# Rounding float64 weights with one VectorE shift and three ScalarE operations, and a subtraction of one moved from VectorE to ScalarE

## The chip, the cores and the metric

The kernel runs on one core of a Trainium2 chip. The metric is the device time of one execution in microseconds (us); three executions of the kernel before were timed, and a fourth was recorded by the hardware profiler. The engines are named as the profile names them: PE is TensorE (PEld its weight loads), DVE is VectorE, ACT is ScalarE, POOL is GpSimd, SP is SyncE, which here only issues DMAs. Each engine takes its instructions in the order in which the program wrote them.

## The reference

Three layers follow one another on 8 sequences of 3072 tokens with 256 channels: a filter in the frequency domain, a soft mixture of experts, and a gated feed-forward layer. Cut to what matters:

```python
X = np.fft.rfft(x, axis=1)
y = np.fft.irfft(X * (filt_r + 1j * filt_i)[None], n=seq, axis=1)      # layer 1
logits = y @ phi                                                       # layer 2
d = softmax(logits over tokens); slot_input = d.T @ y                  # 32 slots, 8 experts
slot_out[e] = relu(slot_input[e] @ w1[e]) @ w2[e]
z = softmax(logits over slots) @ slot_out
g = z @ w_gate                                                         # layer 3
out = (g * sigmoid(g) * (z @ w_val)) @ w_out
```

The three weights of layer 3 (`w_gate`, `w_val`: 256 x 1536; `w_out`: 1536 x 256) are given as float64, everything else as float32. The kernel computes in float32, so these weights are rounded to float32 on the chip.

## The kernel before, in words

**Stage 1** (`phase1`, to about 412 us of the profiled execution) does the transforms. The work is a list of 96 units: 16 steps (a step is one half of the channels of one of the 8 sequences) of 6 units each. For each unit `s2_unit` does 16 matmuls into a PSUM tile `X`, two DVE products `P` and `Q` read from it, and POOL combines them to `y`; two units later `tr_unit` transposes `y` on PE into `T`, ACT copies it to `yt`, and `phi_pair` multiplies with `phi` into `L`. In four of six units `s1_chunk` does a chunk of the next step's first transform: PE writes the PSUM tile `s` (L217), DVE transposes it to `sg` (L225), and `spread` copies that on ACT to `b` (L234), which the next step's `X` matmuls read. The tile `s` has one buffer, so the next chunk's matmuls wait until DVE has read the one before.

Beside the units run two generators, each advanced by one `yield` at a time. `pump` advances `chain(b, last)` by one step a unit: it turns the logits of sequence `b` into slot inputs. Its steps, in order, are `lh` and `us` (evacuations on ACT), `t4` (two transposes on DVE), `lg` (two ACT copies, L396) with `cm` (two DVE reductions L397 and a maximum L398), a PE transpose of `cm` (L407), `mg`, `mb`, `dg` (small DVE operations), `dd` (two DVE subtractions L420 and two ACT exponentials L426), the subtraction of one from `dd` (L430, two on DVE), PE matmuls over `dd` (L438), two DVE transposes to `bd` (L347), PE matmuls over `bd` (L450), and so on. `aside` advances `conv`, two steps a unit, which rounds the weights; when that is used up it advances `first_weights`.

`conv` works on 36 chunks of 128 x 256 weights, four steps a chunk. SP loads a chunk as pairs of 32-bit words into `raw` (two buffers; the load for chunk n+2 is issued behind the store of chunk n). Step 1: DVE takes the exponent `ex` and the mantissa's high part `mn` from the high words (L584, L585). Step 2: ACT scales the exponent, the low words and the mantissa (L587 to L589). Step 3: DVE joins sign and exponent (L591). Step 4: POOL adds and multiplies (L593, L594), and SP stores the result in DRAM and issues the next load.

**Transition and stage 2.** Then the experts run on 32 slots (`transition`, to about 454 us), behind loads of their weights that begin when stage 1 has freed its memory, and stage 2 (`phase2`) does the gated layer to the end.

Of the kernel before, what the change touches and what calls it, by code (L numbers as in the profile page):

```python
# [7 lines left out]
F32 = mybir.dt.float32  # L8
F32R = mybir.dt.float32r
I32 = mybir.dt.int32  # L10
U32 = mybir.dt.uint32
AF = mybir.ActivationFunctionType
ALU = mybir.AluOpType
# [66 lines left out]
def spectral_softmoe_glu_kernel(  # L80
# [18 lines left out]
    pe, dve, act, pool = nc.tensor, nc.vector, nc.scalar, nc.gpsimd  # L99
# [13 lines left out]
    expo = const.tile([128, 1], F32, name="expo")  # L113
# [17 lines left out]
    def phase1():  # L131
        with ExitStack() as c1:
# [5 lines left out]
            cvp = c1.enter_context(tc.tile_pool(name="cvp", bufs=1))  # L138
# [168 lines left out]
            def chain(b, last):  # L307
# [33 lines left out]
                def col(t, k, n=128):  # L341

                    w = 512 // n
                    return t[k // w][:, k % w * n:(k % w + 1) * n]
# [6 lines left out]
                for k in range(6):  # L351
                    pe.transpose(
                        out=col(ps, k),
# [6 lines left out]
                for jj in range(NJ):  # L360
                    g, k = jj % 4, jj // 4
                    pe.matmul(
                        out=col(ps, k)[32 * g:32 * g + 32],
# [23 lines left out]
                for h in range(2):  # L387
                    for g in range(2):
                        pe.matmul(
                            out=pl[h][64 * g:64 * g + 64].rearrange("p (e n) -> p e n", n=16),  # L390
# [9 lines left out]
                for h in range(2):  # L400
                    for g in range(2):
                        nc.sync.dma_start(
                            out=lgd[b].rearrange("(n h) g e k -> h g n e k", h=2)[h, g],
# [6 lines left out]
                    out=mg, in_=ps[0:32, 0:128].rearrange("p (g n) -> p g n", g=2)[:, :, 0:48], axis=AX.X, op=ALU.max  # L410
# [7 lines left out]
                dd = chp.tile([128, 2, E, 16], F32, tag="t4", name="dd")  # L418
                for h in range(2):
                    dve.tensor_tensor(  # L420
                        out=dd[:, h],
                        in0=lg[h],
                        in1=pm[:, :, None].to_broadcast([128, E, 16]),
                        op=ALU.subtract,
# [2 lines left out]
                if not last:  # L427
                    yield
                for h in range(2):
                    dve.tensor_scalar_add(dd[:, h], dd[:, h], -1.0)  # L430
                yield
                bd = chp.tile([128, E, 32], F32, tag="lg", name="bd")
                pl = (ps_s1.tile([128, 1024], F32, tag="s1", name="cl") if last else small()).rearrange(
# [2 lines left out]
                for g in range(2):  # L436
                    for h in range(2):
                        pe.matmul(  # L438
                            out=pl[64 * h:64 * h + 64, g],
# [8 lines left out]
                for jj in range(NJ):  # L448
                    g, k = jj % 4, jj // 4
                    pe.matmul(  # L450
                        out=col(ps, k)[32 * g:32 * g + 32],
# [26 lines left out]
                for q in range(3):  # L478
                    for ri in range(2):
                        for g in range(4):  # L480
                            pe.matmul(  # L481
                                out=ps[32 * g:32 * g + 32, 0:D],
# [17 lines left out]
                if last:  # L500
                    pe.matmul(
                        out=pss[96:128, :], lhsT=rb[:, b, :], rhs=sl, start=False, stop=True, tile_position=(0, 96)
# [52 lines left out]
            def flat(a):  # L555
                return a.rearrange("(p a) f -> p (a f)", p=128)

            def conv():


                cw = 256
                chunks = [(i, c) for i in range(3) for c in range(FF * D // 128 // cw)]
                raws = {}

                def load(n):
                    if n >= len(chunks):
                        return
                    i, c = chunks[n]
                    raws[n] = cvp.tile([128, cw, 2], I32, tag="raw", name="raw", bufs=2)
                    nc.sync.dma_start(  # L570
                        out=raws[n].rearrange("p n k -> p (n k)"),
                        in_=flat((w_gate, w_val, w_out)[i])[:, c * cw:(c + 1) * cw].bitcast(I32),
                    )

                load(0)
                load(1)
                yield
                for n, (i, c) in enumerate(chunks):
                    raw = raws.pop(n)
                    hw, lw, lf = raw[:, :, 1], raw[:, :, 0].bitcast(U32), raw[:, :, 0].bitcast(F32)  # L580
                    ex = cvp.tile([128, cw], I32, tag="ex", name="ex", bufs=2)
                    mn = cvp.tile([128, cw], I32, tag="mn", name="mn", bufs=2)
                    mf = mn.bitcast(F32)
                    dve.tensor_scalar(ex, hw, 20, 0x7FF, ALU.logical_shift_right, ALU.bitwise_and)  # L584
                    dve.tensor_scalar(mn, hw, 0xFFFFF, 0x100000, ALU.bitwise_and, ALU.bitwise_or)  # L585
                    yield
                    act.activation(ex, ex, AF.Relu, bias=expo, scale=float(1 << 23))  # L587
                    act.activation(lf, lw, AF.Copy, scale=2.0 ** -32)
                    act.activation(mf, mn, AF.Copy)  # L589
                    yield  # L590
                    dve.scalar_tensor_tensor(ex, hw, -(1 << 31), ex, ALU.bitwise_and, ALU.bitwise_or)  # L591
                    yield
                    pool.tensor_tensor(out=mf, in0=mf, in1=lf, op=ALU.add)  # L593
                    pool.tensor_tensor(out=mf, in0=mf, in1=ex.bitcast(F32), op=ALU.mult)  # L594
                    nc.sync.dma_start(out=flat(wd[i])[:, c * cw:(c + 1) * cw], in_=mf)
                    load(n + 2)
                    yield
# [54 lines left out]
                        spread()  # L652
            xp += [cr.enter_context(tc.tile_pool(name=f"xp{k}", bufs=1, side="right")) for k in (1, 0)][::-1]
            dve.memset(ones, 1.0)
            dve.memset(expo, -916.0 * (1 << 23))
            side = [conv(), first_weights()]
            todo = []
            gens, ready = [], []
# [18 lines left out]
            def tail_ops(i):  # L677
                if 0 <= i - 2 < len(units):
                    tr_unit(*units[i - 2])
                if i - 4 >= 0 and i % 2 == 0 and i - 3 < len(units):  # L680
                    s, u = units[i - 4]
                    phi_pair(s, u // 2)
                    if s % 2 == 1 and u == 4:
                        ready.append((s // 2, chain(s // 2, s // 2 == NB - 1)))
# [352 lines left out]
    with tc.manual_schedule():  # L1037
        phase1()
        phase2(transition())
        p2.close()  # L1040
# [32 lines left out]
```

## Time and profile before

| | us |
|---|---|
| three timed executions | 1542.36, 1543.30, 1543.52 (median 1543.3) |
| span of the profiled execution | 1537.9 |
| what the median has beyond that span | 5.4 |
| busy in the profiled execution: PE, DVE, ACT, POOL | 1449.9, 1204.9, 955.1, 241.3 |
| end of stage 1, end of the transition | about 412, about 454 |

The profile gives the profiled execution's time as its span alone; the 5.4 us between this and the median of the timed runs lies outside the span. Busy times are averages over stages with different limits, so a change in stage 1 has to be read in stage 1.

### The profile page before, as it was taken

The page shows a single profiled execution, that of the slowest core. Times are in us where ns is not written, and L with a number is a line of the kernel's source. Part 1 is how long each engine was busy: PE and PEld are TensorE (multiplying, and loading weights), DVE is VectorE, ACT ScalarE, POOL GpSimd, SP SyncE. Part 2 cuts the span into 40 slices and gives each one's busy share as a digit, 9 for nine tenths or more (in the row PEclk, how much of TensorE's full clock was granted, in tenths as well). Part 3 has the DMA queues.
Part 4 walks back from the last instruction along what each step waited for, and adds up shares of the span by engine and source line. Part 5 has one row for each costly group of instructions (what it writes and reads, how often), then busy time and mean ns, then how long its engine had stood idle before and what let it go on. Part 6 is the DMA issues. An engine that isn't in the chain of part 4 may idle for free.

```text
span 1537.9 us, 26707 instructions
## 1 busy us (share of the span) xinstructions
PE 1449.9 (94%) x10282; PEld 1133.8 (74%) x10282; DVE 1204.9 (78%) x1976; ACT 955.1 (62%) x1808; POOL 241.3 (16%) x297
## 2 busy tenths in 40 slices
PE   3789998898869999999999999999999999999998
PEld 1455555555438888888888888888888888888887
DVE  3698899898328878887887788788778878877775
ACT  2365565564227666766766677677667667666665
POOL 1566555654010000000000000000000000000000
PEclk9999999999989999999999999999999999999999
DMA  9978678761990120121112013101301310120111
GB/s 193 189 132 147 115 132 142 124 117 56 366 279 25 35 68 19 29 69 27 27 35 71 16 28 69 30 23 35 72 15 29 69 35 18 35 62 14 28 29 28
DMA packets 90482, 116.53 MB, mean 76 GB/s; under 512 B 8657, under 2 KB 69970, under 8 KB 90034
## 3 DMA queue, kind: packets, MB, share of 16 engines
q1 hardware_dynamic: 88882, 111.15, 33.2%
q10 hardware_dynamic: 1216, 3.15, 1.1%
q8 instruction: 81, 1.33, 0.4%
q0 software_dynamic: 256, 0.52, 0.2%
q14 instruction: 47, 0.39, 0.1%
HBM read 68.13 MB, written 34.60 MB: 67 GB/s over the span
## 4 chain that ended last, share of the span: by engine, by line
PE 80%; DVE 11%; DMA 5%; issue 2%; ACT 1%; SPq 1%; POOL 0%; DVEq 0%; ACTq 0%; POOLq 0%
PE o L987 35%; PE o L991 18%; PE V L960 9%; PE G L959 9%; PE X L248 2%; DVE sg L225 2%; DVE P L256 2%; PE s L217 2%; DVE Q L257 2%; DMA fwd<-in_const_fwd_dram 2%; DMA raw<-in_moe_w_gate_dram 1%; PE T L279 1%; PE c L481 1%; DMA w<-in_moe_w_dram 1%; PE L L288 1%
## 5 line engine op out<-in xcount | busy, mean ns | idle before, releaser
L987 PE MATMUL o<-wo,hi 128*128 128x512 f32 x2304 | 831.1, 395 | 0.0
L991 PE MATMUL o<-wo,lo 128*128 128x256 f32 x2304 | 644.6, 280 | 0.2 <-DVE lo L976 0.2
L962 ACT ACTIVATE s<-G 128x512 f32<-128x512 f32 x576 | 344.7, 598 | 317.4 <-PE G L959 314.5
L968 DVE TENSOR_TENSOR h<-V,s 128x512 f32<-128x512 f32 x576 | 395.2, 686 | 168.9 <-ACT s L962 168.1
L987 PEld LDWEIGHTS o<-wo,hi 128*128 128x128 f32 x2304 | 432.0, 187 | 103.4
L991 PEld LDWEIGHTS o<-wo,lo 128*128 128x128 f32 x2304 | 433.6, 188 | 25.9 <-DVE lo L976 0.6
L976 DVE TENSOR_TENSOR lo<-h,hi 128x512 fp32r<-128x512 f32 x576 | 417.1, 724 | 0.1
L975 ACT CAST hi<-h 128x512 fp32r<-128x512 f32 x576 | 354.7, 616 | 12.5 <-DVE h L968 9.2
L960 PE MATMUL V<-c,v 128*128 128x512 f32 x576 | 227.4, 395 | 2.1 <-DVE h L968 1.8
L959 PE MATMUL G<-c,g 128*128 128x512 f32 x576 | 227.9, 396 | 0.0
L248 PEld LDWEIGHTS X<-b,fwd 128*64 128x64 f32 x1536 | 83.2, 138 | 67.9 <-issue 50.2
L959 PEld LDWEIGHTS G<-c,g 128*128 128x128 f32 x576 | 108.1, 188 | 25.6 <-issue 0.8
L234 ACT COPY b<-sg 128x768 f32<-128x768 f32 x64 | 58.7, 918 | 102.6 <-DVE sg L225 102.3
L225 DVE STREAM_TRANSPOSE sg<-s 128x1024 f32<-128x1024 f32 x64 | 78.9, 1236 | 47.9 <-PE s L217 47.9
L248 PE MATMUL X<-b,fwd 128*64 128x128 f32 x1536 | 106.3, 281 | 10.5 <-ACT b L234 5.0
L960 PEld LDWEIGHTS V<-c,v 128*128 128x128 f32 x576 | 108.6, 189 | 4.2 <-DVE h L968 2.9
L906 POOL TENSOR_TENSOR lg<-lg,mx 96x1024 f32<-96x1024 f32 x7 | 16.9, 2418 | 581.1 <-DVE mx L904 581.1
L217 PE MATMUL s<-x,csm 48*64 48x512 f32 x512 | 73.3, 628 | 34.2 <-DMA x<-in_x_dram 21.1
L1001 DVE TENSOR_TENSOR ot<-o,tmp 128x256 f32<-128x256 f32 x192 | 70.0, 423 | 39.5 <-ACT tmp L1000 39.5
L269 POOL TENSOR_TENSOR y<-P 128x256 f32<-128x256 f32 x96 | 70.2, 731 | 144.5 <-DVE P L256 144.5
L271 POOL TENSOR_TENSOR y<-Q 128x256 f32<-128x256 f32 x95 | 77.4, 815 | 0.9 <-DVE Q L259 0.8
L281 ACT COPY yt<-T 128x512 f32<-128x512 f32 x96 | 55.9, 582 | 30.4 <-PE T L279 29.9
(195 smaller groups left out, 1017.6 us busy)
## 6 DMA issues: line engine op xcount, KB each, us to landing
out_dram<-ot SPq DMA_DIRECT2D x192, 128.0 KB, 2.2
x<-in_x_dram SPq DMA_DIRECT2D x56, 384.0 KB, 8.2
w<-in_moe_w_dram SPq DMA_DIRECT2D x16, 1024.0 KB, 12.4
c<-ch SPq DMA_DIRECT2D x42, 128.0 KB, 2.4
c<-cl SPq DMA_DIRECT2D x42, 128.0 KB, 2.4
raw<-in_moe_w_gate_dram SPq DMA_DIRECT2D x12, 256.0 KB, 4.5
lgd<-lg SPq DMA_DIRECT2D x32, 96.0 KB, 6.9
raw<-in_moe_w_val_dram SPq DMA_DIRECT2D x12, 256.0 KB, 3.7
```

The lines of the kernel that those rows point to most:

```text
L217: pe.matmul(out=ps[64 * k:64 * k + 64, 16 * r:16 * r + 16, :], lhsT=s1t_sb[64 * r:64 * r + 48, :], rhs=xt[step][64 * r:64 * r + 48, k, :, ...
L225: dve.transpose(out=sg.rearrange("p j d k -> p d j k"), in_=ps.rearrange("p n d -> p d n"))
L248: pe.matmul(out=ps[par * 64:(par + 1) * 64, i, ri, :], lhsT=fwd[:, j, ri * 64:(ri + 1) * 64], rhs=bb[:, j, :],)
L271: eng.tensor_tensor(out=y[:, :, 1, :], in0=Q[:, :, 0, :], in1=Q[:, :, 1, :], op=ALU.add)
L959: pe.matmul(out=pg, lhsT=g4[c][:, fs], rhs=c4[b][:, q, G, :])
L960: pe.matmul(out=pv, lhsT=v4[c][:, fs], rhs=c4[b][:, q, G, :])
L962: act.activation(s, pg, AF.Silu)
L968: dve.tensor_tensor(out=h, in0=pv, in1=s, op=ALU.mult)
L975: act.copy(hi, h)
L976: dve.tensor_tensor(out=lo, in0=h, in1=hi, op=ALU.subtract)
L987: pe.matmul(out=a, lhsT=hi[:, ts], rhs=wo[f].rearrange("p k d -> p (k d)"), start=(f == 0), stop=(f == NF - 1), skip_group_check=True,)
L991: pe.matmul(out=a[:, D:2 * D], lhsT=lo[:, ts], rhs=wo[f][:, 0, :], start=False, stop=(f == NF - 1), skip_group_check=True,)
```

## The change

The rounding of a chunk is done in another way, still in four steps. Step 1: ACT reads the high words as float32 and scales them, which moves the exponent, into `mag`. Step 2: ACT scales the low words into an integer `low` of 0 to 8, and writes the sign of the high words over them. Step 3: DVE shifts `mag` left by three bits, which drops the old sign. Step 4: POOL adds `low` to `mag` as integers, and multiplies with the sign. So DVE has one operation a chunk and not three, ACT three as before, POOL two as before with an integer add. The subtraction of one in `chain` goes to ACT for the seven sequences that are not the last.

```diff
                 for h in range(2):
-                    dve.tensor_scalar_add(dd[:, h], dd[:, h], -1.0)
+                    if last:
+                        dve.tensor_scalar_add(dd[:, h], dd[:, h], -1.0)
+                    else:
+                        act.activation(dd[:, h], dd[:, h], AF.Copy, bias=-1.0)
                 yield
...
                     raw = raws.pop(n)
-                    hw, lw, lf = raw[:, :, 1], raw[:, :, 0].bitcast(U32), raw[:, :, 0].bitcast(F32)
-                    ex = cvp.tile([128, cw], I32, tag="ex", name="ex", bufs=2)
-                    mn = cvp.tile([128, cw], I32, tag="mn", name="mn", bufs=2)
-                    mf = mn.bitcast(F32)
-                    dve.tensor_scalar(ex, hw, 20, 0x7FF, ALU.logical_shift_right, ALU.bitwise_and)
-                    dve.tensor_scalar(mn, hw, 0xFFFFF, 0x100000, ALU.bitwise_and, ALU.bitwise_or)
-                    yield
-                    act.activation(ex, ex, AF.Relu, bias=expo, scale=float(1 << 23))
-                    act.activation(lf, lw, AF.Copy, scale=2.0 ** -32)
-                    act.activation(mf, mn, AF.Copy)
-                    yield
-                    dve.scalar_tensor_tensor(ex, hw, -(1 << 31), ex, ALU.bitwise_and, ALU.bitwise_or)
-                    yield
-                    pool.tensor_tensor(out=mf, in0=mf, in1=lf, op=ALU.add)
-                    pool.tensor_tensor(out=mf, in0=mf, in1=ex.bitcast(F32), op=ALU.mult)
+                    hf, lw = raw[:, :, 1].bitcast(F32), raw[:, :, 0].bitcast(U32)
+                    mag = cvp.tile([128, cw], I32, tag="mag", name="mag", bufs=2)
+                    low = cvp.tile([128, cw], I32, tag="low", name="low", bufs=2)
+                    act.activation(mag.bitcast(F32), hf, AF.Copy, scale=2.0 ** -112)
+                    yield
+                    act.activation(low, lw, AF.Copy, scale=2.0 ** -29)
+                    act.activation(hf, hf, AF.Sign)
+                    yield
+                    dve.tensor_scalar(mag, mag, 3, None, ALU.logical_shift_left)
+                    yield
+                    pool.tensor_tensor(out=low, in0=mag, in1=low, op=ALU.add)
+                    mf = low.bitcast(F32)
+                    pool.tensor_tensor(out=mf, in0=mf, in1=hf, op=ALU.mult)
                     nc.sync.dma_start(out=flat(wd[i])[:, c * cw:(c + 1) * cw], in_=mf)
```

On DVE, this is the stretch of one sequence's chain from `cm` to the transpose behind `dd`, before and then after; the numbers on `s` tell one tile from the next.

```order
L584 TENSOR_SCALAR ex<-raw 128x256
L585 TENSOR_SCALAR mn<-raw 128x256
L397 TENSOR_REDUCE cm<-lg 128x32 x2
L398 TENSOR_TENSOR cm<-cm 128x32
L256 TENSOR_TENSOR P<-X,ft 128x512
L257 TENSOR_TENSOR Q<-X,ft 128x512
L591 SCALAR_TENSOR_TENSOR ex<-raw,ex 128x256
```

```order
L397 TENSOR_REDUCE cm<-lg 128x32 x2
L398 TENSOR_TENSOR cm<-cm 128x32
L256 TENSOR_TENSOR P<-X,ft 128x512
L257 TENSOR_TENSOR Q<-X,ft 128x512
L591 TENSOR_SCALAR mag<-mag 128x256
L409 TENSOR_REDUCE mg<-c 32x2
```

The pair `ex`, `mn` ahead of `cm` is gone, and the shift stands where the join of sign and exponent stood, directly behind `Q`.

Further on in the same chain, on DVE, from `dg` to the transposes `bd`, before and then after:

```order
L414 TENSOR_SCALAR dg<-csm,mb 32x32
L225 STREAM_TRANSPOSE sg<-s_2226 128x32x16x2
L256 TENSOR_TENSOR P<-X,ft 128x512
L257 TENSOR_TENSOR Q<-X,ft 128x512
L584 TENSOR_SCALAR ex<-raw 128x256
L585 TENSOR_SCALAR mn<-raw 128x256
L420 TENSOR_TENSOR dd<-lg,c 128x512 x2
L225 STREAM_TRANSPOSE sg<-s_2279 128x32x16x2
L256 TENSOR_TENSOR P<-X,ft 128x512
L257 TENSOR_TENSOR Q<-X,ft 128x512
L591 SCALAR_TENSOR_TENSOR ex<-raw,ex 128x256
L430 TENSOR_SCALAR dd<-dd 128x512 x2
```

```order
L414 TENSOR_SCALAR dg<-csm,mb 32x32
L225 STREAM_TRANSPOSE sg<-s_2190 128x32x16x2
L256 TENSOR_TENSOR P<-X,ft 128x512
L257 TENSOR_TENSOR Q<-X,ft 128x512
L420 TENSOR_TENSOR dd<-lg,c 128x512 x2
L225 STREAM_TRANSPOSE sg<-s_2242 128x32x16x2
L256 TENSOR_TENSOR P<-X,ft 128x512
L257 TENSOR_TENSOR Q<-X,ft 128x512
L591 TENSOR_SCALAR mag<-mag 128x256
L225 STREAM_TRANSPOSE sg<-s_2277 128x32x16x2
```

One `ex`, `mn` pair ahead of `dd` and both subtractions ahead of the next `sg` are gone.

On ACT at the same place, before and then after:

```order
L426 ACTIVATE dd<-dd 128x512 x2
L587 ACTIVATE ex<-ex,expo 128x256
L588 ACTIVATE raw<-raw 128x256
L589 ACTIVATE mn<-mn 128x256
L234 COPY b<-sg 128x24x32
L281 COPY yt<-T 128x512
L234 COPY b<-sg 128x24x32
```

```order
L586 ACTIVATE mag<-raw 128x256
L426 ACTIVATE dd<-dd 128x512 x2
L588 ACTIVATE low<-raw 128x256
L589 ACTIVATE raw<-raw 128x256
L234 COPY b<-sg 128x24x32
L281 COPY yt<-T 128x512
L433 ACTIVATE dd<-dd 128x512 x2
L234 COPY b<-sg 128x24x32
```

The scaling into `mag`, the first reader of the loaded `raw`, now stands on ACT ahead of the exponentials, and the two subtractions stand between `yt` and the next `b`. Nothing else changes its place on PE, POOL or SP.

## Rows read from the trace of the kernel before

**Rows 1.** The page, its first line.

```profile
span 1537.9 us, 26707 instructions
```

**Rows 2.** Windows: length, busy us (instructions) by engine, clock, DMA; one repeat, five summed.

```profile
177.99:224.03 46.04, 41.74 (x541) 24.94 (x537) 42.11 (x71) 26.69 (x58) 27.01 (x37) 1.00 0.81 135
...
sum 230.21, PE 208.72 PEld 124.76 DVE 210.89 ACT 133.89 POOL 135.45; mean PE 41.74 PEld 24.95 DVE 42.18 ACT 26.78 POOL 27.09
```

**Rows 3.** PE's waits in four repeats, 131.93 to 316.10 us.

```profile
PE s L217 <- DVE sg L225: 6.3, 4, 1.6
PE c L450 <- DVE bd L347: 4.2, 4, 1.0
PE c L407 <- DVE cm L398: 4.0, 4, 1.0
PE X L248 <- ACT b L234: 1.9, 4, 0.5
```

**Rows 4.** PE in order of time, one repeat: start, us, what, idle before.

```profile
188.61 0.27 PE L407 MATMUL c<-csm,cm 128*32 128x128 f32 x1 [1.01 <-DVE cm L398]
...
196.61 1.09 PE L217 MATMUL s<-x,csm 48*64 48x512 f32 x8 [1.57 <-DVE sg L225]
```

**Rows 5.** DVE in order of time, the same repeat.

```profile
186.97 1.27 DVE L397 TENSOR_REDUCE cm<-lg 128x32 f32<-128x512 f32 x2
188.27 0.19 DVE L398 TENSOR_TENSOR cm<-cm 128x32 f32<-128x32 f32 x1
...
193.04 0.42 DVE L584 TENSOR_SCALAR ex<-raw 128x256 int32<-128x256 int32 x1
193.38 0.82 DVE L585 TENSOR_SCALAR mn<-raw 128x256 int32<-128x256 int32 x1
194.12 1.27 DVE L420 TENSOR_TENSOR dd<-lg,c 128x512 f32<-128x512 f32 x2
...
198.15 1.83 DVE L430 TENSOR_SCALAR dd<-dd 128x512 f32<-128x512 f32 x2
```

**Rows 6.** ACT in order of time, the same repeat.

```profile
186.06 1.07 ACT L396 COPY lg<-c 128x512 f32<-128x512 f32 x2 [0.65 <-PE c L389]
...
197.80 0.57 ACT L281 COPY yt<-T 128x512 f32<-128x512 f32 x1
```

**Rows 7.** By tile: durations in ns (min/median/max), first and last start.

```profile
L584 DVE TENSOR_SCALAR ex<-raw x36: 275/498/799, 55.9 to 324.1; 128x256 int32<-128x256 int32 x36
L585 DVE TENSOR_SCALAR mn<-raw x36: 279/818/833, 56.1 to 324.3; 128x256 int32<-128x256 int32 x36
L588 ACT ACTIVATE raw<-raw x36: 414/428/450, 56.6 to 325.5; 128x256 f32<-128x256 uint32 x36
L591 DVE SCALAR_TENSOR_TENSOR ex<-raw,ex x36: 556/570/579, 57.5 to 327.7; 128x256 int32<-128x256 int32 x36
L593 POOL TENSOR_TENSOR mn<-mn,raw x36: 722/737/920, 58.6 to 328.8; 128x256 f32<-128x256 f32 x36
...
L426 ACT ACTIVATE dd<-dd x16: 629/629/633, 102.7 to 399.5; 128x512 f32<-128x512 f32 x16
```

**Rows 8.** SP in order of time: one issue of a load of raw.

```profile
185.97 0.33 SPq L570 DMA_DIRECT2D raw<-in_moe_w_val_dram  x1
```

**Rows 9.** By tile: the landings of raw's loads issued from 90 to 330 us.

```profile
DMA to landing us min/median/max: 2.7/3.9/7.6
```

**Rows 10.** PE in order of time, the end of stage 1.

```profile
333.61 1.09 PE L217 MATMUL s<-x,csm 48*64 48x512 f32 x8 [0.46 <-DVE sg L225]
...
342.17 1.09 PE L248 MATMUL X<-b,fwd 128*64 128x128 f32 x16 [0.31 <-ACT b L234]
...
369.74 1.59 PE L438 MATMUL c<-dd,csm 48*64 48x512 f32 x8 [0.25 <-DVE dd L430]
```

**Rows 11.** DVE in order of time, the start of stage 1.

```profile
75.54 0.29 DVE L584 TENSOR_SCALAR ex<-raw 128x256 int32<-128x256 int32 x1 [1.79 <-DMA raw<-in_moe_w_gate_dram]
```

**Rows 12.** Chain of waits behind stage 1: start, us, what.

```profile
418.90 17.78 DMA w<-in_moe_w_dram
```

More of the change, by code (lines that the diff above doesn't have):

```diff
@@ L654, in phase1 @@
             dve.memset(ones, 1.0)
-            dve.memset(expo, -916.0 * (1 << 23))
+            dve.memset(expo, 0.0)
             side = [conv(), first_weights()]
```

## The prediction

> **What bounds the kernel now.** Two engines are edited, DVE and ACT, and every edited instruction lies in stage 1 or at its end, so I looked at the busy time by window there. One sequence (two steps, 12 units) repeats every 46.04 us, and five such repeats lie one behind the other from 85.9 to 316.1 us [rows 2]. In a repeat PE is busy 41.74 us and DVE 42.1: neither is full, and both are near it, which means that they take turns. The waits of PE say where. In four repeats PE waits in the same four places, once or so in each repeat [rows 3]: for `sg` ahead of a chunk of `s` (6.3 us, 1.58 a repeat), for `bd` (4.2, 1.05), for `cm` (4.0, 1.0) and for `b` ahead of the next step's first `X` (1.9, 0.47). That is 4.1 us a repeat. The order of time shows all four between 188 and 207 us of the repeat drawn here, where the chain's DVE work meets `conv`'s [rows 4, 5]; in the rest of the repeat PE has no wait in its rows and DVE waits for it. So DVE time taken away in that half of a repeat shortens the kernel, until PE's waits there are used up; DVE time taken away elsewhere is worth nothing.
>
> **What is behind stage 1.** The loads of the experts' weights start when stage 1 has freed its memory, and one of them ends the chain there [rows 12]. It is late because stage 1 ends late, so I take what stage 1 gains to arrive at the end one for one. Stage 2 is not touched.
>
> **Prices.** `ex` and `mn` go: 36 of each, median 498 and 818 ns. The join L591 (570) becomes a shift of the same 128 x 256 tile [rows 7]. No row shows the shift. Below, it is like the fastest `ex` (275, half of the join's time); above, like the slowest (799). `ex` is the nearest row, since it is the same kind of instruction on the same shape and stood directly behind `Q`, where the shift stands now; I take 0.5, about what the join took. So the exchange of join for shift is worth 0, between +0.3 and -0.25 us for each.
>
> The Trainium skill speaks against this price ("SBUF — State Buffer", section "SBUF: two separate sides"): VectorE and GpSimd share a port pair that is an exclusive lock, held for a whole instruction by whichever comes first, for VectorE instructions in a 2-port mode or with two SBUF inputs. By that rule a shift that meets POOL's work on `P` would wait for a whole POOL operation; with POOL's 0.74 us for this shape this is 1.0 us and not 0.5, and the sum below would be smaller by 0.5 us a repeat, 2.5 in all. The rows bear the rule out only in part: `ex` and `mn` do spread from 275 to over 800, but the join, which has two SBUF inputs, never left 556 to 579.
>
> On ACT three operations of a chunk replace three. For `mag`, `low` and the sign I take the row of the low words, which reads and writes every second word: 428 [rows 7]; bounds 0.4 and 0.52 (the dearest of the old three), so at worst 0.3 us a chunk on an engine that is busy 26.7 of 46.0 us [rows 2]. The two subtractions on ACT have the exponential's shape and engine: 629 each [rows 7]. POOL's integer add has no row: from below 0.72, the fastest float add, which I take; from above see the rivals.
>
> **The sum for one repeat**, in the order of PE's waits.
>
> 1. `cm`. The ACT copies of `lg` end at 186.06 + 1.07 = 187.13 [rows 6], but DVE, held by `mn`, starts `cm` at 186.97 and ends at 188.46 [rows 5]. Without `mn` the second reduction starts when the second copy ends, at about 187.15; with half of 1.27 and the maximum's 0.19 that is 188.0, 0.45 earlier. PE's wait of 1.01 [rows 4] becomes 0.55. The rest is the latency from PE over ACT and DVE back to PE, which the change doesn't touch. `mag` runs on ACT ahead of the copies, in the 0.65 us in which ACT waits there [rows 6].
> 2. `sg`. From `cm` to that `sg` DVE has no gap, and the pair `ex`, `mn` takes 193.04 to 194.12, or 1.08 [rows 5]. So `sg` is ready 0.45 + 1.08 = 1.53 earlier, while PE gets there 0.45 earlier: its wait falls by 1.08 from 1.57 to about 0.5.
> 3. `bd` and `b`. The subtractions (198.15 to 199.98, of which some 1.75 hold the `sg` behind them) and one more pair (0.9) leave DVE. These 2.65 us exceed the two waits together, 1.05 + 0.47 = 1.52. Both go to zero, and from there PE is full.
>
> That is 0.45 + 1.08 + 1.52 = 3.05 us a repeat, of the 4.1. Five repeats: 15.2 us.
>
> The subtractions on ACT are hidden if they are done before L438. The `yt` copy ahead of them ends at 198.37 [rows 6], 1.5 us earlier in the new time: 196.85. Two subtractions make that 198.1. PE reaches L438, 3.2 us behind the `s` at 196.61, 1.53 earlier too, at 198.3. The cover is thin, 0.2 us; when it is gone, L438 waits for ACT, at up to 0.5 us a repeat.
>
> `mag` on ACT, not `ex` on DVE, now waits for the load of `raw`. The load issued at 185.97 [rows 8] is wanted by the `ex` at 193.04, 7.1 us later; in the new time by `mag` on ACT about 6.4 later. Landings take 3.9 as a median and 7.6 at most [rows 9], so a late one can hold ACT for about a microsecond, with the copies `b` and `yt` behind it, and only a few of 36 do.
>
> **Ends of stage 1.** At the start `raw` comes late: at 75.54 DVE has waited 1.79 us for it [rows 11]. The landing stays; what waits is ACT, and DVE can do `P`, `Q` and `sg` meanwhile. Between 0.3 and 2.5 us gained; I take 1.5. In the last repeat with `conv` the waits of 0.46 and 0.31 [rows 10] go, and 0.45 at `cm` as above: 1.2. For the seventh sequence nothing lies between the exponentials and L438, which already waits 0.25 for the second subtraction [rows 10]. On DVE the first subtraction ran beside the second exponential; on ACT both come behind it, 0.63 each. That loses 0.5.
>
> Sum: 15.2 + 1.5 + 1.2 - 0.5 = 17.4 us. The profiled span of 1537.9 [rows 1] would be 1520.5. What lies around it is 5.4 us up to the median of the runs, 1543.3, and I leave that as it is: **1525.9 us**, or 1.1% less.
>
> **Rivals.**
>
> *All of PE's waits go.* If the latencies in steps 1 and 2 are shorter than I made them, PE is full: 4.1 x 5 + 2.5 + 1.2 = 24 us, 1519. Against it: steps 1 and 2 leave one half microsecond each by the rows. Chance 0.07.
>
> *ACT takes the place of DVE.* ACT has idle time on the average, but it is in order: the two subtractions and late loads of `raw` stand ahead of `b` and `yt`. With the 0.5 us at L438, a 0.5 us wait for `b`, and a shift of 0.8 ahead of `sg` in place of 0.5, a repeat gains 1.75: 8.7 + 1.5 = 10 us, 1533. For it: the cover of 0.2. Chance 0.2.
>
> *The integer add is slow.* POOL is busy 27.0 of 46.04 us a repeat with six chunks [rows 2]. Until an add takes about 3.2 us the loads of `raw`, issued behind it, still land before `mag` wants them (6.4 less 3.9 is 2.5 us over the 0.74 of now). POOL's other work in a repeat is 27.0 - 6 x 0.74 = 22.6, so it fills the new repeat of 43.0 at 3.4 us an add, and the old one, where the gain is gone, at 3.9, a little over five times the float add. At 4.5 us a repeat would be 22.6 + 6 x 4.5 = 49.6: 3.6 us more than now, and the kernel some 20 us slower, 1563. For it: no row of POOL with integers. Against it: a POOL operation that only reads and writes other bits at five times the price would be strange. Chance 0.04.
>
> *The sign calls for another table on ACT.* Each change between it and the exponential would cost a load. The built program has no such load in stage 1 beyond the first, on ACT's list of instructions. Chance under 0.01, left out.
>
> *Nothing comes of it*, because the loads behind stage 1 run to their own clock: they are issued when stage 1 frees memory, so I give it 0.02, at 1543.
>
> **Numbers.** The forecast holds 0.67, with 1522 to 1530 as its own range (shift 0.275 or 0.8, start 0.3 or 2.5). The range reaches into the rivals on both sides, 1519.5 to 1533, and leaves out about 0.2. A measurement of this kernel tells about 0.2% from no change: 3 us. Faster by more than that: 0.67 + 0.07 + 0.2 = 0.94, less a little for what I have not seen, 0.92; within it 0.03; slower 0.05.
>
> **What would show it.** In the trace after: a repeat of 43.0 us with PE busy as before and DVE about 33 of it (42.1, less 10.6 for three operations on six chunks and 1.8 for the subtractions, plus six shifts); PE's waits for `bd` and `b` gone, those for `cm` and `sg` near 0.5; no wait of PE for the subtractions on ACT; shifts at 0.28 to 0.8; integer adds near 0.74; stage 1 ending some 17 us earlier, and the same distance from there to the end. Repeats near 44.3 with PE waiting for ACT would show the second rival, POOL busy over 40 us a repeat the third.

## The result

| | before | changed |
|---|---|---|
| median of the timed runs, us | 1543.41 (1542.36 to 1545.49) | 1522.62 (1520.53 to 1524.18) |
| ratio, with its 95% interval | | 0.9861 (0.9847 to 0.9875) |
| span of the profiled execution, us | 1537.9 [rows 1] | 1521.0 |

The changed kernel is 1.4% faster; 1525.9 us had been forecast, with 1519.5 to 1533. Medians and spans do not agree: the medians lie 20.8 us apart and the profiled spans 16.9. In every timed execution whose span was recorded, time and span differ by 1.7 to 2.0 us, mostly 1.8, not by the 5.4 that the prediction put around the span. So the profiled execution of the kernel before would have been timed at 1539.7: it was a quick one among executions whose spans went from 1537.9 to 1543.8. The granted clock goes with part of this: of the 23 timed executions of the kernel before with a span on record, the 8 whose mean clock was 0.989 or more average 1539.7 us of span, the other 15, with 0.983 to 0.987, average 1542.0; the profiled one had 0.991. All eight of the changed kernel had 0.988 or more, the profiled one 0.990.

### The profile page after: what moved, and what is told of

It is laid out like the page before. It is cut to its first block, busy times and chain, and to the rows that moved or that the text cites. A ratio compares the mean times of both kernels' runs of the same rounds, so it can differ in the third digit from the quotient of the medians.

```text
span 1521.0 us, 26593 instructions
## 1 busy us (share of the span) xinstructions
PE 1449.3 (95%) x10282; PEld 1134.2 (75%) x10282; DVE 1154.6 (76%) x1890; ACT 960.9 (63%) x1822; POOL 234.6 (15%) x297
## 4 chain that ended last, share of the span: by engine, by line
PE 86%; DMA 5%; DVE 5%; ACT 1%; issue 1%; SPq 1%; POOL 0%; DVEq 0%; ACTq 0%; POOLq 0%
PE o L988 35%; PE o L992 18%; PE V L961 9%; PE G L960 9%; PE X L248 3%; PE s L217 3%; PE T L279 2%; DMA raw<-in_moe_w_gate_dram 2%; DMA fwd<-in_const_fwd_dram 2%; PE L L288 1%; PE c L484 1%; DVE sg L225 1%; DMA w<-in_moe_w_dram 1%; DVE cm L397 1%; DVE P L256 1%
## 5 line engine op out<-in xcount | busy, mean ns | idle before, releaser
L992 PEld LDWEIGHTS o<-wo,lo 128*128 128x128 f32 x2304 | 433.6, 188 | 25.9 <-DVE lo L977 0.6
L907 POOL TENSOR_TENSOR lg<-lg,mx 96x1024 f32<-96x1024 f32 x7 | 16.9, 2410 | 580.9 <-DVE mx L905 580.9
L256 DVE TENSOR_TENSOR P<-X,ft 128x512 f32<-128x512 f32 x96 | 63.6, 663 | 20.0 <-PE X L248 18.7
```

The lines of the kernel that those rows point to most:

```text
L256: dve.tensor_tensor(out=P, in0=ps, in1=f, op=ALU.mult)
L992: pe.matmul(out=a[:, D:2 * D], lhsT=lo[:, ts], rhs=wo[f][:, 0, :], start=False, stop=(f == NF - 1), skip_group_check=True,)
```

## The profile after

First line of the page, and the busy time by window of the same five repeats (length, then busy us and instructions of PE, PEld, DVE, ACT, POOL; granted clock, DMA), the third of them and the sum:

```profile
span 1521.0 us, 26593 instructions
```

```profile
171.04:213.38 42.34, 41.15 (x537) 24.84 (x533) 33.56 (x57) 27.46 (x59) 25.87 (x37) 1.00 0.78 143
...
sum 211.74, PE 205.79 PEld 124.21 DVE 167.95 ACT 137.32 POOL 129.39; mean PE 41.16 PEld 24.84 DVE 33.59 ACT 27.46 POOL 25.88
```

A repeat takes 42.35 us and not 46.04 [rows 2]. DVE is busy 33.6 us of it (33 had been forecast, 42.1 before), ACT 27.5 (26.7), POOL 25.9 (27.0). What waits of PE are left is in its list over four repeats (128.69 to 298.08 us; total, times, longest):

```profile
PE c L407 <- ACT yt L281: 2.9, 4, 0.7
PE s L217 <- DVE sg L225: 1.3, 4, 0.3
```

Of the four waits of before [rows 3] those for `bd` and `b` are gone, the one for `sg` fell from 1.58 to 0.33 a repeat, and the one ahead of L407 from 1.0 to 0.72. PE in order of time, where these waits stood:

```profile
180.18 0.66 PE L279 MATMUL T<-csm,y 128*128 128x128 f32 x4
181.56 0.27 PE L407 MATMUL c<-csm,cm 128*32 128x128 f32 x1 [0.73 <-ACT yt L281]
...
187.33 0.66 PE L279 MATMUL T<-csm,y 128*128 128x128 f32 x4
188.32 1.09 PE L217 MATMUL s<-x,csm 48*64 48x512 f32 x8 [0.33 <-DVE sg L225]
...
191.52 1.09 PE L441 MATMUL c<-dd,csm 48*64 48x512 f32 x8
192.43 1.04 PE L217 MATMUL s<-x,csm 48*64 48x512 f32 x8
193.40 1.09 PE L248 MATMUL X<-b,fwd 128*64 128x128 f32 x16
194.42 0.66 PE L279 MATMUL T<-csm,y 128*128 128x128 f32 x4
195.01 1.55 PE L453 MATMUL c<-fwd,bd 128*32 128x128 f32 x48
196.49 1.09 PE L248 MATMUL X<-b,fwd 128*64 128x128 f32 x16
```

The view names ACT's `yt` (180.91 to 181.49) as what ended the wait ahead of L407, but it is still `cm`: DVE ends it at 181.41, and L407 starts 0.15 us later, as it did before (188.46 and 188.61). DVE in order of time there:

```profile
179.91 1.28 DVE L397 TENSOR_REDUCE cm<-lg 128x32 f32<-128x512 f32 x2 [0.72 <-ACT lg L396]
181.22 0.19 DVE L398 TENSOR_TENSOR cm<-cm 128x32 f32<-128x32 f32 x1
```

Each start's distance from the start ahead of it, before less after, gives where the 3.70 us of a repeat come from (`T` is the matmuls L279 ahead of the wait):

| from one start to the next | before | after | gained |
|---|---|---|---|
| `T` to L407 (for `cm`) | 1.67 | 1.38 | 0.29 |
| `T` to `s` (for `sg`) | 2.23 | 0.99 | 1.24 |
| matmuls over `dd` to `s` to `X` | 2.40 | 1.88 | 0.52 |
| `T` to the matmuls over `bd` | 1.69 | 0.59 | 1.10 |
| these to `X` (for `b`) | 2.03 | 1.48 | 0.55 |

The third line is in no list of PE's waits. In the kernel before, PE in order of time has these groups in this part of the repeat:

```profile
186.94 0.66 PE L279 MATMUL T<-csm,y 128*128 128x128 f32 x4
...
194.38 0.66 PE L279 MATMUL T<-csm,y 128*128 128x128 f32 x4
...
199.81 1.30 PE L438 MATMUL c<-dd,csm 48*64 48x512 f32 x8
201.19 1.09 PE L217 MATMUL s<-x,csm 48*64 48x512 f32 x8
202.21 1.09 PE L248 MATMUL X<-b,fwd 128*64 128x128 f32 x16
203.24 0.66 PE L279 MATMUL T<-csm,y 128*128 128x128 f32 x4
204.93 1.55 PE L450 MATMUL c<-fwd,bd 128*32 128x128 f32 x48 [1.04 <-DVE bd L347]
206.96 1.09 PE L248 MATMUL X<-b,fwd 128*64 128x128 f32 x16 [0.47 <-ACT b L234]
```

and the weight loads have this one, with the wait ahead of it:

```profile
201.19 0.21 PEld L217 LDWEIGHTS s<-x,csm 48*64 48x64 f32 x8 [0.96 <-DVE sg L225]
```

The eight matmuls took 1.30 us as a group there and 1.09 after; the `s` behind them had to wait for `sg`, which only the weight load's row says. PE's busy time of a repeat was 41.74 and is 41.16: what looked like work was in part a wait.

The prices, for the tile `mag` and those made from it (min/median/max in ns, first and last start):

```profile
L586 ACT ACTIVATE mag<-raw x36: 435/447/473, 57.5 to 305.6; 128x256 f32<-128x256 f32 x36
L591 DVE TENSOR_SCALAR mag<-mag x36: 294/441/457, 58.0 to 309.6; 128x256 int32<-128x256 int32 x36
L593 POOL TENSOR_TENSOR low<-mag,low x36: 717/726/732, 58.4 to 310.5; 128x256 int32<-128x256 int32 x36
```

and for the tile `dd`:

```profile
L433 ACT ACTIVATE dd<-dd x14: 613/630/652, 105.0 to 351.5; 128x512 f32<-128x512 f32 x14
```

The shift takes 0.44 as a median and never over 0.46; the integer add is no dearer than the float add (0.737); the subtraction on ACT is the exponential's 0.63.

## The experiments

The theory is that of the prediction: what counts is DVE time on its gapless way through one half of a repeat, until PE is full there. The length of a repeat, from one sequence's L362 to the next in the profile, is the finest measure: most repeats of one execution agree within 0.05 us, and the table names those that don't, while whole times move by some us from one execution to the next. Where there is only one execution, it is the measure.

| run | repeat, us | time, us | ratio to before |
|---|---|---|---|
| before | 46.04 | 1543.4 | |
| changed | 42.35 | 1522.6 | 0.986 (0.985 to 0.988) |
| rounding alone | 43.43 | 1527.4 | 0.990 (0.988 to 0.992) |
| subtraction alone | 44.38 (later four; first 45.37) | 1535.8 | 0.995 (0.993 to 0.996) |
| idle pair in the chain's half | 43.50 (second 43.83) | 1526.7 (one) | |
| idle pair in the other half | 42.35 (second 42.68) | 1522.4 (one) | |
| idle pair in all chunks | 43.84 (fifth 44.08) | 1528.7 (one) | |
| idle operation on ACT | 42.35 | 1523.7 (one) | |
| seventh sequence on DVE | 42.35 | 1521.9 (one) | |
| maximum from PSUM | 43.1 (first two), then 44.2 | 1531.8 | 0.992 (0.989 to 0.995) |
| maximum first | 42.25 | 1523.2 | 0.987 (0.985 to 0.989) |
| changed, again | 42.35 | 1521.7 | 0.987 (0.985 to 0.988) |

The first repeat of the subtraction alone is longer because the granted clock was 0.96 in it and 1.00 in the next two.

**Each part alone.** The subtractions go back to DVE in the changed kernel, and to ACT in the kernel before.

```diff
# rounding alone, against the changed kernel
-                    if last:
-                        dve.tensor_scalar_add(dd[:, h], dd[:, h], -1.0)
-                    else:
-                        act.activation(dd[:, h], dd[:, h], AF.Copy, bias=-1.0)
+                    dve.tensor_scalar_add(dd[:, h], dd[:, h], -1.0)
# subtraction alone, against the kernel before: the same lines the other way round
```

> The changed kernel with the subtractions of one back on DVE for all sequences; the rounding stays new. Theory (DVE time in the chain's half of a repeat is what counts, until PE has no wait left): some 1.8 us of DVE work come back between L420 and bd, where DVE now waits for PE, so most is hidden: a repeat of 42.4 to 43.0 us against 42.35 in the changed kernel, and the seventh sequence gets its 0.5 us back; time 1522 to 1526. Rival (the subtractions carry about half of the gain): a repeat near 44.2, time near 1531.

> The kernel before with the subtractions on ACT; the rounding stays old. Theory: 1.75 us of DVE work leave the stretch in which PE waits for sg, bd and b behind L438, which together hold about 2.1 us of PE's waits: a repeat of 44.3 to 44.5 us against 46.04, time near 1535. So this and the rounding alone gain more than both together. Rival (DVE is the bound of the whole repeat and each part gives its share of removed DVE time, 1.8 of some 8.5 us): a repeat near 45.3, time near 1539.

The rounding alone gains 2.61 us a repeat, the subtraction alone 1.66, together 4.27, and the two in one kernel 3.70. So they share waits, as the theory has it, and DVE's total is not the measure: by that the subtraction would have given some 0.8, its 1.8 of the 8.5 us of DVE time that left a repeat, times 3.70. But the rounding alone missed its window (42.4 to 43.0): I had held most of the subtractions to be hidden behind DVE's wait for PE. PE in order of time in that run:

```profile
190.63 1.16 PE L438 MATMUL c<-dd,csm 48*64 48x512 f32 x8
191.87 1.09 PE L217 MATMUL s<-x,csm 48*64 48x512 f32 x8
...
196.69 1.09 PE L248 MATMUL X<-b,fwd 128*64 128x128 f32 x16 [0.46 <-ACT b L234]
```

From L438 to `s` it takes 1.24 and not 0.91, and `b` is waited for again: with two subtractions of 0.95 us DVE has no gap on its way to the last `sg` of the step. Of their 1.8 us 1.1 show in the repeat.

**DVE time put back, here or there.** Two operations on constants, which nobody waits for, stand where `ex` and `mn` stood, in two of six chunks.

```diff
                     act.activation(mag.bitcast(F32), hf, AF.Copy, scale=2.0 ** -112)
+                    if n % 6 in (5, 0):     # the other half: (2, 3); all chunks: no condition
+                        idle = cvp.tile([128, 192], I32, tag="idle", name="idle")
+                        dve.tensor_scalar(idle, csm[:, 0:192].bitcast(I32), 20, 0x7FF, ALU.logical_shift_right, ALU.bitwise_and)
+                        dve.tensor_scalar(idle, csm[:, 0:192].bitcast(I32), 0xFFFFF, 0x100000, ALU.bitwise_and, ALU.bitwise_or)
                     yield
```

> The changed kernel with two idle integer operations on DVE (128x192, on constants, written to a tile that nobody reads) where ex and mn stood, for those two of six chunks of a repeat whose pair stood ahead of cm and ahead of dd. They depend on nothing. Theory (DVE time at this place): the pair ahead of dd is on DVE's gapless way to sg, so PE's wait for sg of 0.33 grows by the pair's 0.5 to 1.0; the pair ahead of cm is hidden in DVE's wait for ACT or costs up to 0.4. A repeat of 42.9 to 43.7. Rival (what counted was that raw, ex and mn were waited for, not DVE's time): 42.35, no change.

> The changed kernel with the same idle pairs for the two of six chunks whose pair stood in the other half of a repeat, where PE has no wait. Theory (place decides): a repeat of 42.35 to 42.4, no change, though DVE has the same busy time as with the pairs in the chain's half. Rival (DVE's total decides): the same repeat as with the pairs in the chain's half.

> The changed kernel with the idle pair on DVE (three quarters of the width of ex and mn) in step 1 of all 36 chunks. Nobody waits for it. Theory (the rounding's share of the gain is DVE time and nothing else): about the repeat of the kernel with the old rounding and the subtractions on ACT, 44.4 us, less some tenths for the smaller width: 43.9 to 44.4. Rival (what the new rounding saves is also the waiting of DVE for raw and of ACT for ex): 43.5, as with the pairs in the chain's half alone.

Twelve pairs of about 1.0 us each cost 1.15 us a repeat in one half and nothing in the other. In both runs the second repeat is 0.33 longer than the rest: DVE pauses there for 0.24 us between `cm` and `P`, which the profile ties to no releaser, and since both have it, it leaves the difference alone. PE's waits over the same stretch (130 to 300 us), first with the pairs in the chain's half:

```profile
PE s L217 <- DVE sg L225: 5.8, 4, 1.7
PE c L407 <- DVE cm L398: 3.3, 4, 0.8
```

and with the pairs in the other half:

```profile
PE c L407 <- ACT yt L281: 2.9, 4, 0.7
PE s L217 <- DVE sg L225: 1.6, 4, 0.7
```

In the first, PE's wait for `sg` is longer than in the changed kernel by 1.1 us, about the pair's own length. With pairs in all chunks the repeat is 43.84, just below its window; the old rounding with the subtractions on ACT took 44.38. The 0.5 us between them are not settled: the idle operations have three quarters of the width, and the old join took 0.57 where the shift takes 0.44, three times on the way. DVE time on constants thus gives back 1.49 of the 2.03 us that separate the two roundings there. The rival that saw the gain in the waiting for `raw` has at most the rest.

**Room on ACT.**

```diff
                     act.activation(mag.bitcast(F32), hf, AF.Copy, scale=2.0 ** -112)
+                    idle = cvp.tile([128, 192], F32, tag="idle", name="idle")
+                    act.activation(idle, csm[:, 0:192], AF.Copy)
```

> The changed kernel with one more idle operation on ACT in step 1 of every chunk (128x192, from a constant to a tile that nobody reads, about 0.35 us). Theory (ACT has room, and its last operation ahead of L441 ends 0.7 us before PE gets there): repeat 42.35 to 42.5. Rival (ACT in order is near to taking the place of DVE): each of the three ahead of L441 delays cm, sg or L441 by its length, repeat 42.7 to 43.4.

The repeat is the same to the hundredth, with 36 more operations of 0.36 us. ACT has room for them at this place, and the rival is refuted there.

**The seventh sequence.** Its subtractions stay on DVE.

```diff
-                    if last:
+                    if b >= NB - 2:
                         dve.tensor_scalar_add(dd[:, h], dd[:, h], -1.0)
```

> The changed kernel, but the subtractions of the seventh sequence, behind the last conv chunk, on DVE as before. Theory: PE's wait of 0.81 us ahead of that sequence's L441 falls to about 0.25, and the stretch from that sequence's start to the last sequence's maximum shortens by 0.5; the five repeats stay at 42.35. Rival (the wait is made up for behind it, by waits for first_weights): no change of that stretch.

PE in order of time, the changed kernel and then this one:

```profile
351.65 1.60 PE L441 MATMUL c<-dd,csm 48*64 48x512 f32 x8 [0.81 <-ACT dd L433]
```

```profile
350.38 1.59 PE L441 MATMUL c<-dd,csm 48*64 48x512 f32 x8 [0.25 <-DVE dd L431]
```

The wait is back to 0.25, and the stretch from that sequence's L362 to the last sequence's L407 took 41.33 us against 41.83. This stretch scatters as a whole (42.67 in the changed kernel run again), but not its first part: from that L362 to the `T` ahead of which PE waits 1.49 us it took 26.65 and 26.64 in the two profiles of the changed kernel, 26.65 with the idle operation on ACT, and 26.31 here. So 0.34 of the expected 0.5 is shown. The rest of the 0.56 is made up for behind it, 0.15 of that at a wait for DVE's `Q` (0.71, now 0.86).

**The wait that is left ahead of L407.** First the maximum is taken from PSUM, then also ahead of the copies, both with the seventh sequence's subtractions on DVE.

```diff
# maximum from PSUM
                 for h in range(2):
                     act.copy(lg[h], pl[h].rearrange("p (e n) -> p e n", n=16))
-                    dve.tensor_reduce(out=cm[:, h], in_=lg[h], axis=AX.X, op=ALU.max)
+                    dve.tensor_reduce(out=cm[:, h], in_=pl[h].rearrange("p (e n) -> p e n", n=16), axis=AX.X, op=ALU.max)
# maximum first: both reductions, then their maximum, then both copies
```

> As the run with the seventh sequence's subtractions on DVE, and in addition DVE takes the maximum cm from the PSUM tile itself, not from ACT's copy of it. Theory (what is left of PE's wait ahead of the transpose of cm is the way from PE over ACT to DVE and back): DVE starts 0.6 us earlier, that wait falls from 0.73 to 0.1 to 0.3, the repeat to 41.7 to 41.9, and the last two sequences gain as much: 3 to 4 us less than the changed kernel, 1518 to 1520. Rival (the wait for sg, which is DVE's own length from cm on, takes over or DVE and ACT hinder each other in PSUM): repeat 42.2 or more.

> As the run with the maximum from PSUM, but DVE's two reductions over the PSUM tile are written ahead of ACT's two copies of it, so that their reads of the one tile no longer take turns. Theory (in that run each reader waited for the reader before it, DVE for ACT and ACT for DVE): DVE starts at the end of L389, PE's wait ahead of the transpose of cm is 0 to 0.2 us, the clock stays at its upper level in all repeats, a repeat of 41.6 to 41.9 us, and 1517 to 1520 in all. Rival (reads of one PSUM tile by two engines cost even so, or the copies that are now late hold up dd or ACT): a repeat above 42.2.

Both missed, in two ways. With the maximum from PSUM, ACT in order of time has

```profile
140.65 0.58 ACT L396 COPY lg<-c 128x512 f32<-128x512 f32 x1 [0.31 <-PE c L389]
141.99 0.59 ACT L396 COPY lg<-c 128x512 f32<-128x512 f32 x1 [0.76 <-DVE cm L397]
```

DVE has

```profile
141.26 0.69 DVE L397 TENSOR_REDUCE cm<-c 128x32 f32<-128x512 f32 x1 [0.71 <-ACT lg L396]
142.61 0.69 DVE L397 TENSOR_REDUCE cm<-c 128x32 f32<-128x512 f32 x1 [0.65 <-ACT lg L396]
```

and PE, behind both,

```profile
143.67 0.27 PE L409 MATMUL c<-csm,cm 128*32 128x128 f32 x1 [1.48 <-DVE cm L400]
```

In this program the two readers of one PSUM tile take turns, each waiting for the reader before it, even where the halves of the tile differ. The Trainium skill says that accesses of two engines at once to the same PSUM bank and the same 32 partitions, reads included, are a collision, and that a bank is 2 KiB of a partition ("PSUM — Partial Sum Buffer", the entry on the PSUM bank). Each half here, 512 float32 values, is as large as one bank, and the rows show ACT's copy of the second half held up by DVE's reduction of the first all the same; what two readers cost without these waits was not tested. PE's wait doubled to 1.48.

With the reductions first, PE in order of time has

```profile
181.40 0.28 PE L409 MATMUL c<-csm,cm 128*32 128x128 f32 x1 [0.96 <-ACT lg L400]
```

DVE has

```profile
178.89 1.29 DVE L397 TENSOR_REDUCE cm<-c 128x32 f32<-128x512 f32 x2
180.21 0.19 DVE L398 TENSOR_TENSOR cm<-cm 128x32 f32<-128x32 f32 x1
```

and ACT

```profile
180.27 1.07 ACT L400 COPY lg<-c 128x512 f32<-128x512 f32 x2 [1.68 <-DVE cm L397]
```

`cm` is ready at 180.40, 1.0 us ahead of L409 and, counted from L389, 0.6 earlier than in the changed kernel, but the transpose L409 writes a new tile in the one buffer `c`, and that is free only when ACT has copied `lg` from it, at 181.34. The wait for `sg` is gone and the one ahead of L409 grew to 0.96: a repeat gains 0.1, and the whole time cannot be told from the changed kernel's. No version here is faster than the changed kernel beyond what a measurement tells.

**The changed kernel again.**

> The changed kernel once more, to stand beside the run with the maximum first on the same chip and to see how far the start of stage 1 moves from one execution to the next. Theory: five repeats of 42.35 us, the first repeat's begin within 2 to 3 us of 86.3, time 1520 to 1524. Rival: the repeats themselves move.

The repeats are 42.35 again; the first begins at 83.9 us, against 86.3 in the first profile. Over the runs with the new rounding and no idle work on DVE this point lies between 83.3 and 86.3, apart from the run with the maximum from PSUM, where it was 89.3; with the old rounding it was 85.7 and 86.1.

## Why the prediction was right, step by step

*What bounds the kernel.* Right: PE and DVE take turns, and the half decides. The same idle work costs 1.15 us a repeat in one half and nothing in the other.

*The sum for a repeat.* The mechanism was right, the size short: 3.70 and not 3.05. Step 1 was too high (0.29 for 0.45): the second reduction starts not with the end of the second copy (180.36) but 0.15 later, since DVE is still at the first. Step 2 was too low (1.24 for 1.08): between `cm` and `sg` the shift is also some 0.14 shorter than the join, an exchange that the prediction took to be worth nothing. Step 3 was too low (1.65 for 1.52), and 0.52 us behind the matmuls over `dd` were missing. That wait for `sg` was hidden in PE's busy time, and I had read only PE's list of waits, not the weight loads'.

*Prices.* Shift 0.44 (0.5 taken), integer add 0.73 (0.72), operations of ACT 0.43 to 0.45 (0.43), subtraction 0.63 (0.63): right. The Trainium skill's rule of the exclusive port ("SBUF — State Buffer", "SBUF: two separate sides") would have made the shift 1.0 by the prediction's reading, that it waits for a whole POOL operation; the rows say at most 0.46. POOL and then DVE in order of time:

```profile
182.09 0.73 POOL L269 TENSOR_TENSOR y<-P 128x256 f32<-128x256 f32 x1 [2.10 <-DVE P L256]
```

```profile
182.53 0.44 DVE L591 TENSOR_SCALAR mag<-mag 128x256 int32<-128x256 int32 x1
```

The shift starts 0.44 us behind POOL's operation and ends 0.15 behind its end, so it can have waited for no more than what was left of it. This fits the rule without proving it, and so does an idle operation in the other half: at 157.08, 0.15 behind the start of POOL's work on `Q`, it took 0.76 and ended 0.11 behind it, where its pair's second took 0.26.

*Hidden work.* The subtractions on ACT end 0.7 us before PE wants them, where 0.2 had been worked out; the rival in which ACT takes DVE's place falls with the idle operation that cost nothing.

*Ends of stage 1.* At the start 1.5 us had been taken. ACT now waits for `raw`, as forecast, and DVE doesn't:

```profile
77.12 0.45 ACT L586 ACTIVATE mag<-raw 128x256 f32<-128x256 f32 x1 [4.19 <-DMA raw<-in_moe_w_gate_dram]
```

But the first repeat began 0.6 us later in the first profile after and 1.8 us earlier in the second: the term is smaller than the scatter of the loads at the start, and stays open. The last repeat with `conv` gained 0.8 (1.2 forecast). From the seventh sequence's L362 to the last L407 1.3 us were lost, not 0.5. At L441 PE waits 0.56 longer, as worked out, of which 0.33 are left at the `T` with the wait of 1.49; the other 0.97 were lost behind it, where PE's first three rows from 365.6 us on took 1.08 to 1.12 us in place of 0.63 to 0.73, at a granted clock of 0.63 up to 370.0 (last section). From the last L407 to the end it is 1141.2 us before and 1141.7 after, so what stage 1 gains arrives at the end but for 0.5.

*What lies around the span.* This was the wrong term: 1.8 us and not 5.4. With 1.8 the same sum gives 1522.3, so this term alone is more than the 3.3 us by which the forecast lies above the measured time. That the medians differ by 20.8 and the profiles by 16.9 is because the profiled execution of before was quicker than its median by some 3.7 us. Part of this goes with the granted clock, as the result shows; where in an execution it is won or lost was not found.

*Where the sum was lucky.* The profiles differ by 16.9 us, near to the 17.4 worked out, but two errors cancel. Five repeats gained 18.5 and not 15.2, and what lies around them lost 1.6 (0.6 at the start, 1.3 at the seventh sequence and 0.5 behind it, less 0.8 gained in the last repeat with `conv`), where a gain of 2.2 had been forecast.

## What to carry to other kernels

When two engines take turns, find the half in which the one has no gap, and price only what leaves that half: here the same work cost 1.15 us a repeat in one half and nothing in the other, and two parts that end the same waits gave 2.61 and 1.66 alone but 3.70 together. Read the weight loads' waits beside the matmuls' own, since a wait in the middle or at the end of a group of matmuls can look like busy time. Before a reader is moved to PSUM for a shorter way, ask who else reads that tile and who wants its buffer next.

## What was not expected of the hardware

In the run with the maximum from PSUM, where PE waits 1.48 us once a repeat, the first two repeats took 43.1 us and the later ones 44.2. The windows of the fourth repeat, up to the end of the wait at 231.05 and from 1 us behind it:

```profile
222.00:231.00 9.00, 7.43 (x86) 4.84 (x82) 7.14 (x13) 5.84 (x13) 4.30 (x6) 1.00 0.19 56
...
232.00:236.20 4.20, 4.20 (x34) 2.46 (x30) 3.33 (x8) 1.49 (x3) 3.78 (x6) 0.59 1.26 135
```

The granted clock, 1.00 up to 232.0, is 0.59 on the mean over the next 4.2 us, which is mostly the lower of its two levels (1.2 GHz), and then 1.00 again; such a repeat is 1.1 us longer. Of this kernel's four times, 1527.2 and 1529.1 came with a mean clock of 0.987 and 0.986, 1534.5 and 1536.0 with 0.984 and 0.983. The first two repeats had the same wait and kept the clock, and so did the kernel before with a wait of 1.57 at another place [rows 4], so the wait alone does not decide it. A drop of the same kind met the changed kernel between 365.6 and 370.0 us (0.63), behind waits of 1.49 and 0.82 us; the kernel before has the same two waits at the same place, at 382.45 and 383.90, and there the matmuls behind them took 0.63 to 0.73 us. Why one wait is followed by a drop and another isn't was not tested.
